# W1's splits wait for batch 5, and the planned order of the work is drawn up anew

## The chip, the core and the metric

The kernel runs on one core of one Trainium2 chip. The metric is the device time of one execution in microseconds (us), as the median of three runs. The core's engines are PE (TensorE, matrix products), DVE (VectorE), ACT (ScalarE), POOL (GpSimd) and SP (SyncE), which issues the transfers (DMA). Each engine works its own queue in order; they wait for each other through semaphores.

## What is computed

Attention of 8 batches with 8 heads, 512 tokens and 32 states each, in both directions, then two MLPs on the 4608 results of width 512, all in float32:

```python
scores = scale * np.matmul(x, state.transpose(0, 1, 3, 2))
a = np.exp(scores - scores.max(-1, keepdims=True))
a /= a.sum(-1, keepdims=True) + 1e-09
xread = np.matmul(a, state)
...                                       # the same with state and x exchanged: sread
x = concatenate([xread, sread]) as 8 * (512 + 32) tokens of 512
h = x @ w_in                              # first MLP, 512 -> 1024: W1
solu = h * softmax(h)
ln = (solu - mean) / np.sqrt(var + 1e-06) * g_ln
y = ln @ w_out                            # 1024 -> 512: W2
h = y @ moe2_w_in                         # second MLP, 512 -> 2048: W3
g = h * (1.0 / (1.0 + np.exp(-1.702 * h)))
return g @ moe2_w_out                     # 2048 -> 512: W4
```

## The kernel before

The weights come as 64-bit numbers. `to_f32` (line 440) turns a block of 128 x 512 into float32: a load of 512 KB to a raw tile, two passes on ACT, three on DVE (lines 453, 456 and 458) and an integer addition on POOL (line 460). Products of full precision are made from three products of reduced precision. For that `split` (line 463) copies a tile to a high part `hi` (line 472 on ACT or line 474 on DVE) and subtracts it to a low part `lo` (line 467, on POOL or DVE).

Batches 0 to 7 don't apply W1 to their tokens. Per batch, `attention` transposes x and the state, forms the scores, and takes a softmax over the states: subtraction of maxima m1 (line 595), exponential, sums z1, multiplication (line 602), a transposition to aT (line 605), and a split of aT to `ahi`, `alo` (line 609). The state is multiplied by W1 (`state_w1`, line 566 on PE, split to `vhi`, `vlo`, lines 656 and 657), which uses W1 as float32 and not its splits. So the first product of the first MLP (`mlp1`) of a batch is `ahi`, `alo` against `vhi`, `vlo` (lines 431 to 433 on PE). The other softmax, over tokens, begins with lines 575 to 585 and line 620. Line 710 takes the row maximum of h, line 712 the exponential, line 714 the product u, and lines 724 and 725 scale it. The output product with W2 takes `zhi`, `zlo` (`z_T`, lines 766 to 774; `z_turn`, line 755, from batch 3 on).

What comes from the other direction, 256 tokens of state reads, is batch 8. For these alone W1 is split, to eight pairs `hi_w1s`, `lo_w1s`. Meanwhile W3 is prepared for seven products per block in place of eight (`prepare_up`): four conversions, sums of blocks, seven splits, and stores of these to DRAM; from there the second MLP, 400 us and later, loads them.

The order is not that of the code. Each piece of work is a step with an engine or a choice of engines, a cost, and for some a due time (`key`). A planner runs once, on paper: it passes due times back along the dependences, keeps a time for each engine, and picks the next step among those whose inputs and buffers are there, by the earliest start and then by the earliest due time. Constants say how far ahead loads may go (`LOOK`, `LEAD`), how many buffers stay free (`KF`, `KR`, `RK`, `KEEP`), when a second engine is preferred (`MARGIN`, `LOAD`), how long an early step may be passed over (`WAIT`), and the due times of the parts (`W1DUE`, `ATT`, `M1A`, `M2A`, `SLOT` and others). The instructions are then issued to each engine in the order so found. The chip has no part in it, and waits are real semaphore waits.

The splits of W1 have a due time near batch 7, but nothing keeps the planner from taking them when an engine has nothing more urgent by its own reckoning:

```python
W1s[k, f] = split(W1[k, f], f"w1s_{k}_{f}", b * SLOT - 10 + k + KD * f)
```

Float32 tiles of 128 x 512 share 71 buffers, raw tiles of W1 seven, raw tiles of the other weights two.

Of the kernel before, what the change touches and what calls it, by code (L numbers as in the profile page):

```python
# [15 lines left out]
ALU = mybir.AluOpType  # L16
# [6 lines left out]
ZB = 3  # L23
XD = 3
AHEAD = 30.092
KF = 10.181
LOOK = 27.681
KR = 0.745
STEPS = 13.000
LATEV = 99  # L30
HEADS = 1.060
W1S = 20.477
ATT = -0.468
ZL = 7.738
M1B = -7.631
VST = 25.191
RK = 8
LEAD = 62.849
KEEP = 5
PP = 1.33  # L40
FIRST = "dz"

# [42 lines left out]
class Plan:  # L85
# [88 lines left out]
    def plan(self):  # L174
# [19 lines left out]
        while ready:  # L194
# [4 lines left out]
            for s in ready:  # L199
                e0 = s.eng[0][0]  # L200
                if e0 == "pe" and s.key > front + AHEAD:
                    continue
                if e0 == "dma" and s.due > front + (LEAD if s.keep else LOOK):
                    continue
# [5 lines left out]
                for k, n in need.items():  # L210
# [115 lines left out]
            self.late.release()  # L326


WAIT = 43.673
W1DUE = -10.782  # L330
MARGIN = 19.804
M1A = -3.168
M1S = 14.618
M2A = 48.714
M2S = 3.142
A1 = 4.656
DMAQ = 0
STQ = "dma"
WARM = 7
LD = 1.875  # L340
LA = -0.409
LOAD = dict(dve=LD, act=LA)
COLD = 18.042
IDLE = 2.200
XRAW = 1
BUS = 347350.590

BUS0 = 170067.709
BUS0T = 8.428
PAIR = 14.200  # L350
HOLDM = 2.261
HOLDW = 9.169
HOLD = dict(m=HOLDM, w=HOLDW)


@with_exitstack
def attention_solu_gelu(ctx: ExitStack, tc: tile.TileContext, x, state, w1, w2, g_ln, w3, w4, out):
    nc = tc.nc
    B, H, S, D = x.shape
# [8 lines left out]
    KD = DM // P  # L368
# [4 lines left out]
    scale = 1.0 / float(D) ** 0.5  # L373
    NX = B * NS
    PSUM = bass.MemoryType.PSUM
    SLOT = 40.392

    const = ctx.enter_context(tc.tile_pool(name="const", bufs=1))
    slot_p = ctx.enter_context(tc.tile_pool(name="slots", bufs=1))
# [5 lines left out]
    do, tl = pl.do, pl.tile  # L385
# [21 lines left out]
    def POOL(c):  # L407
        return [("pool", c)]
# [28 lines left out]
    TOP = 122879.9921875  # L437
    TINY = 2.0 ** -15

    def to_f32(src, name, due, after=(), keep=0, kind="r"):  # L440

        raw = tl(kind, [P, 512, 2], U32, f"raw_{name}")
        do(ACT(.1) if kind == "d" and DMAQ else DMA(), lambda e: e.dma_start(out=raw().rearrange("p f w -> p (f w)").bitcast(U64), in_=src),
           writes=[raw], key=due - 4, nbytes=P * 4096, after=after)
        w = tl("s", [P, 512], F32, f"w_{name}")

        def u():
            return w().bitcast(U32)  # L450

        do(ACT(.52), lambda e: e.activation(w(), raw()[:, :, 1].bitcast(F32), AF.Abs), [raw], [w], keep=keep)
        do(DVE(.335), lambda e: e.tensor_scalar(w(), w(), TINY, TOP, op0=ALU.max, op1=ALU.min), [w], [w])
        do(ACT(.52), lambda e: e.activation(raw()[:, :, 0], raw().bitcast(U16)[:, :, 1], AF.Copy, scale=2.0 ** -13),
           [raw], [raw])
        do(DVE(.335), lambda e: e.tensor_scalar(u(), u(), 3, 0x3FFFFFF8, op0=ALU.logical_shift_left,
                                                op1=ALU.bitwise_and), [w], [w])
        do(DVE(.6), lambda e: e.scalar_tensor_tensor(out=u(), in0=raw()[:, :, 1], scalar=0xC0000000, in1=u(),  # L458
                                                     op0=ALU.bitwise_and, op1=ALU.bitwise_or), [raw, w], [w])
        do(POOL(1.23), lambda e: e.tensor_tensor(u(), u(), raw()[:, :, 0], op=ALU.add), [w, raw], [w], key=due)  # L460
        return w

# [51 lines left out]
    def attention(b):  # L514
# [734 lines left out]
```

## Time and profile before

| | |
|---|---|
| runs | 1113.74, 1111.53, 1110.18 us |
| median | 1111.53 us |
| profiled execution, its own time | 1111.82 us |
| its span, first to last instruction | 1110.0 us |
| granted clock of TensorE, mean | 0.988 |
| PE busy | 1070.6 us, 96% |
| DVE, ACT, POOL busy | 808.5, 616.2, 248.3 us |

The profiled execution took 1111.82 us, 1.8 more than the span from its first to its last instruction. Busy time is the time in which an engine works on instructions; what is left of a window is idle. A wait is put down to the instruction that released it. A short form such as "x4" says that four like instructions stand one behind the other, with the time from the first's start to the last's end.

### The profile page before, as it was taken

How to read it: one execution, taken by the hardware profiler on the slowest of the kernel's cores; microseconds unless marked ns; L12 is line 12 of the kernel's file. 1: busy time of each engine (PE TensorE's matmuls, PEld its weight loads, DVE VectorE, ACT ScalarE, POOL GpSimd, SP SyncE). 2: the span in 40 equal slices, each digit the busy share in tenths (PEclk: the TensorE clock that was granted, in tenths of full speed). 3: DMA queues.
4: the chain of work that ended last, by engine and by line, in shares of the span. 5: the costliest groups of instructions: out<-in, count | busy, mean ns of one | idle time of the engine just before them, and what ended most of it. 6: DMA issues, size and time to landing. Idle time of an engine off the chain costs nothing.

```text
span 1110.0 us, 22067 instructions
## 1 busy us (share of the span) xinstructions
PE 1070.6 (96%) x8255; PEld 966.4 (87%) x8255; DVE 808.5 (73%) x1374; ACT 616.2 (56%) x1111; POOL 248.3 (22%) x212
## 2 busy tenths in 40 slices
PE   6689999999899999999999999999999999999998
PEld 3357777767577789999999999999999999999998
DVE  5999767898878838548866665435498888778874
ACT  6587555667557547557756665545354444444441
POOL 3977432651836502310101110000000000000000
PEclk8899999999999999999999999999999999999999
DMA  7314352866754479998776657479934344434521
GB/s 231 81 51 100 84 111 70 231 153 156 201 114 108 158 210 361 336 365 305 243 240 235 216 205 250 160 256 392 375 107 152 104 126 146 129 108 152 152 78 58
DMA packets 233084, 202.81 MB, mean 183 GB/s; under 512 B 128784, under 2 KB 174864, under 8 KB 232976
## 3 DMA queue, kind: packets, MB, share of 16 engines
q1 hardware_dynamic: 232880, 201.26, 57.8%
q8 instruction: 65, 1.06, 0.4%
q14 instruction: 43, 0.35, 0.1%
q10 hardware_dynamic: 96, 0.13, 0.1%
HBM read 113.25 MB, written 82.84 MB: 177 GB/s over the span
## 4 chain that ended last, share of the span: by engine, by line
PE 79%; DVE 6%; SPq 4%; POOL 4%; DMA 2%; issue 2%; ACT 2%; POOLq 0%; DVEq 0%; ACTq 0%
PE psum L1039 10%; PE psum L1037 10%; PE psum L950 10%; PE psum L1038 10%; PE psum L951 10%; PE psum L949 10%; PE psum L431 5%; PE psum L433 5%; PE psum L432 5%; DMA raw_w<-in_moe_w_in 2%; POOL lo_w3s L467 2%; SPq L745 1%; PE psum L766 1%; PE psum L566 1%; DVE w_w L458 1%
## 5 line engine op out<-in xcount | busy, mean ns | idle before, releaser
L1037 PE MATMUL psum<-w4r,hi_g 128*128 128x256 f32 x896 | 252.2, 282 | 0.0
L1039 PE MATMUL psum<-w4r,lo_g 128*128 128x256 f32 x896 | 252.1, 281 | 0.0
L1038 PE MATMUL psum<-w4r,hi_g 128*128 128x256 f32 x896 | 251.9, 281 | 0.0
L1037 PEld LDWEIGHTS psum<-w4r,hi_g 128*128 128x128 f32 x896 | 169.3, 189 | 0.0
L1038 PEld LDWEIGHTS psum<-w4r,hi_g 128*128 128x128 f32 x896 | 169.3, 189 | 0.0
L1039 PEld LDWEIGHTS psum<-w4r,lo_g 128*128 128x128 f32 x896 | 169.2, 189 | 0.0
L472 ACT CAST hi_g<-a_g 128x512 fp32r<-128x512 f32 x128 | 77.9, 620 | 108.5 <-DVE a_g L819 54.6
L460 POOL TENSOR_TENSOR w_w<-w_w,raw_w 128x512 uint32<-128x512 uint32 x48 | 68.7, 1436 | 295.0 <-DVE w_w L458 188.2
L431 PE MATMUL psum<-zhi,hi_w 128*128 128x512 f32 (+1 forms) x288 | 115.6, 401 | 1.5 <-DVE u L714 1.5
L961 DVE TENSOR_TENSOR c<-psum,u 128x512 f32<-128x512 f32 x64 | 44.1, 690 | 92.5 <-PE psum L951 57.3
L433 PE MATMUL psum<-zhi,lo_w 128*128 128x512 f32 (+1 forms) x288 | 110.1, 382 | 0.0
L896 DVE TENSOR_TENSOR lo_g<-a_g,hi_g 128x512 fp32r<-128x512 f32 x128 | 86.0, 687 | 16.9 <-PE psum L1039 8.3
L472 ACT CAST hi_g<-gr 128x512 fp32r<-128x512 f32 x104 | 63.0, 619 | 47.4 <-PE psum L1038 21.8
L933 ACT ACTIVATE t<-c 128x512 f32<-128x512 f32 x96 | 60.5, 632 | 46.6 <-DVE c L961 43.0
L896 DVE TENSOR_TENSOR lo_g<-gr,hi_g 128x512 fp32r<-128x512 f32 x104 | 71.0, 687 | 13.9 <-ACT hi_g L472 8.3
L432 PE MATMUL psum<-zlo,hi_w 128*128 128x512 f32 (+1 forms) x208 | 78.2, 376 | 0.0
L431 PEld LDWEIGHTS psum<-zhi,hi_w 128*128 128x128 f32 x288 | 54.5, 189 | 23.3 <-issue 9.2
L433 PEld LDWEIGHTS psum<-zhi,lo_w 128*128 128x128 f32 x288 | 54.4, 189 | 11.2
L950 PE MATMUL psum<-lo_x,w3r_2h 128*128 128x256 f32 x224 | 63.0, 281 | 0.0
L950 PE MATMUL psum<-lo_x,w3r_3h 128*128 128x256 f32 x224 | 63.0, 281 | 0.0
L951 PE MATMUL psum<-hi_x,w3r_3l 128*128 128x256 f32 x224 | 63.0, 281 | 0.0
L951 PE MATMUL psum<-hi_x,w3r_0l 128*128 128x256 f32 x224 | 62.9, 281 | 0.0
(233 smaller groups left out, 3004.4 us busy)
## 6 DMA issues: line engine op xcount, KB each, us to landing
g<-t SPq DMA_DIRECT2D x136, 256.0 KB, 3.7
gr<-g SPq DMA_DIRECT2D x136, 256.0 KB, 3.3
w4r<-w4k SPq DMA_DIRECT2D x56, 256.0 KB, 5.3
raw_w<-in_moe_w_in SPq DMA_DIRECT2D x24, 512.0 KB, 5.7
raw_w<-in_moe_w_out SPq DMA_DIRECT2D x24, 512.0 KB, 4.9
xb<-scr SPq DMA_DIRECT2D x34, 256.0 KB, 5.0
scr<-x SPq DMA_DIRECT2D x16, 512.0 KB, 4.0
out<-oc SPq DMA_DIRECT2D x32, 256.0 KB, 2.7
```

The costliest lines, as they stand in the source:

```text
L431: nc.tensor.matmul(o, lhi, rhi, start=first, stop=False)
L432: nc.tensor.matmul(o, lhi, rlo, start=False, stop=False)
L433: nc.tensor.matmul(o, llo, rhi, start=False, stop=last)
L460: do(POOL(1.23), lambda e: e.tensor_tensor(u(), u(), raw()[:, :, 0], op=ALU.add), [w, raw], [w], key=due)
L472: e.copy(o, i)
L896: do(DVE(.68), lambda e: e.tensor_tensor(flat_(lo), flat_(t), flat_(hi), op=ALU.subtract), [t, hi], [lo], key=due)
L949: nc.tensor.matmul(o, wh()[:, k, cut], hi()[:, k, :], start=first and not mi + k, stop=False, **OPEN)
L950: nc.tensor.matmul(o, wh()[:, k, cut], lo()[:, k, :], start=False, stop=False, **OPEN)
L951: nc.tensor.matmul(o, wl()[:, k, cut], hi()[:, k, :], start=False, stop=bool(mi and k), **OPEN)
L1037: nc.tensor.matmul(o, hi()[:, mi, cut], wt[:, 0], start=first, stop=False, **OPEN)
L1038: nc.tensor.matmul(o, hi()[:, mi, cut], wt[:, 1], start=False, stop=False, **OPEN)
L1039: nc.tensor.matmul(o, lo()[:, mi, cut], wt[:, 0], start=False, stop=2 * j + mi == NM - 1 and u == 1, **OPEN)
```

## The change

Three edits. The function `split` gets a list of steps that its high part must wait for, and W1's splits are given the last product of batch 5's first MLP (`last` holds the last product of each batch, and B is 8). The last addition of `to_f32` can be put on a choice of engines, and both constants that say so name POOL, as before. And 28 of the planner's constants have other values, of which three stand here.

```diff
-LOOK = 27.681
+LOOK = 37.674
-WAIT = 43.673
+WAIT = 31.914
-MARGIN = 19.804
+MARGIN = 14.062
...
+ADD = ("pool",)
+ADD1 = ("pool",)
...
-    def to_f32(src, name, due, after=(), keep=0, kind="r"):
+    def to_f32(src, name, due, after=(), keep=0, kind="r", add=ADD):
...
-        do(POOL(1.23), lambda e: e.tensor_tensor(u(), u(), raw()[:, :, 0], op=ALU.add), [w, raw], [w], key=due)
+        do([(q, dict(pool=1.23, dve=.6)[q]) for q in add], lambda e: e.tensor_tensor(u(), u(), raw()[:, :, 0], op=ALU.add),
+           [w, raw], [w], key=due)
...
-    def split(w, name, due, shape=(512,), pair=None, low=(("pool", 1.23), ("dve", .6))):
+    def split(w, name, due, shape=(512,), pair=None, low=(("pool", 1.23), ("dve", .6)), after=()):
...
-        do([("act", .52), ("dve", .335)], lambda e: copy(e, hi(), w()), [w], [hi])
+        do([("act", .52), ("dve", .335)], lambda e: copy(e, hi(), w()), [w], [hi], after=after)
...
-                    W1s[k, f] = split(W1[k, f], f"w1s_{k}_{f}", b * SLOT - 10 + k + KD * f)
+                    W1s[k, f] = split(W1[k, f], f"w1s_{k}_{f}", b * SLOT - 10 + k + KD * f, after=[last[B - 3]])
```

The changed lines shift the numbers of those behind them by two or three: line 460 of before is line 462, 467 is 470, 595 is 598, 602 is 605, 609 is 612, 724 and 725 are 727 and 728.

Both kernels have 4468 steps, and nearly all keep their engine; it is their order that differs. Three places of POOL's queue show it. The first is the start of batch 0's softmax and the second half of W1 (`w_w1_k_f` is block k of half f; `s1_0_0` is batch 0's softmax, its first half). Before:

```order
L595 TENSOR_TENSOR s1_0_0_375<-s1_0_0_375,m1_0_0_471 128x512
L595 TENSOR_TENSOR s1_0_1_384<-s1_0_1_384,m1_0_1_479 128x512
L467 TENSOR_TENSOR lo_w1s_0_0_512<-w_w1_0_0_339,hi_w1s_0_0_473 128x512
L467 TENSOR_TENSOR lo_w1s_1_0_521<-w_w1_1_0_354,hi_w1s_1_0_486 128x512
L467 TENSOR_TENSOR lo_w1s_2_0_534<-w_w1_2_0_361,hi_w1s_2_0_504 128x512
L467 TENSOR_TENSOR lo_w1s_3_0_553<-w_w1_3_0_386,hi_w1s_3_0_541 128x512
L460 TENSOR_TENSOR w_w1_0_1_414<-w_w1_0_1_414,raw_w1_0_1_312 128x512
L460 TENSOR_TENSOR w_w1_1_1_450<-w_w1_1_1_450,raw_w1_1_1_316 128x512
L460 TENSOR_TENSOR w_w1_2_1_458<-w_w1_2_1_458,raw_w1_2_1_320 128x512
L460 TENSOR_TENSOR w_w1_3_1_508<-w_w1_3_1_508,raw_w1_3_1_372 128x512
L602 TENSOR_TENSOR s1_0_0_375<-s1_0_0_375,z1_0_0_566 128x512
```

The same place after:

```order
L598 TENSOR_TENSOR s1_0_0_383<-s1_0_0_383,m1_0_0_463 128x512
L598 TENSOR_TENSOR s1_0_1_394<-s1_0_1_394,m1_0_1_466 128x512
L462 TENSOR_TENSOR w_w1_0_1_451<-w_w1_0_1_451,raw_w1_0_1_309 128x512
L462 TENSOR_TENSOR w_w1_1_1_454<-w_w1_1_1_454,raw_w1_1_1_311 128x512
L462 TENSOR_TENSOR w_w1_2_1_459<-w_w1_2_1_459,raw_w1_2_1_316 128x512
L462 TENSOR_TENSOR w_w1_3_1_515<-w_w1_3_1_515,raw_w1_3_1_380 128x512
L605 TENSOR_TENSOR s1_0_0_383<-s1_0_0_383,z1_0_0_538 128x512
L605 TENSOR_TENSOR s1_0_1_394<-s1_0_1_394,z1_0_1_543 128x512
L612 TENSOR_TENSOR alo0_0_577<-aT0_0_561,ahi0_0_563 128x512
L612 TENSOR_TENSOR alo0_1_587<-aT0_1_573,ahi0_1_583 128x512
```

The four low parts between the subtractions (line 595, now 598) and the additions of W1's second half are gone, and the low part of batch 0's softmax, `alo0`, stands directly behind the multiplications.

The second is the first block of W3 (`w_w3_0010` is a converted part of it, `u3_2` a row tile of batch 3). Before, the first two additions stand behind batch 4's `alo`:

```order
L609 TENSOR_TENSOR alo4_0_2234<-aT4_0_2216,ahi4_0_2225 128x512
L725 TENSOR_SCALAR u3_2_2043<-u3_2_2043,sml3_2_2033 128x1024
L609 TENSOR_TENSOR alo4_1_2261<-aT4_1_2228,ahi4_1_2237 128x512
L460 TENSOR_TENSOR w_w3_0010_2038<-w_w3_0010_2038,raw_w3_0010_1917 128x512
L460 TENSOR_TENSOR w_w3_0011_2083<-w_w3_0011_2083,raw_w3_0011_1926 128x512
L724 TENSOR_TENSOR sml3_3_2199<-sml3_3_2199,half_p_80 128x1
L725 TENSOR_SCALAR u3_3_2244<-u3_3_2244,sml3_3_2199 128x1024
```

After, they stand among the scalings of batch 2:

```order
L727 TENSOR_TENSOR sml2_2_1606<-sml2_2_1606,half_p_80 128x1
L728 TENSOR_SCALAR u2_2_1632<-u2_2_1632,sml2_2_1606 128x1024
L462 TENSOR_TENSOR w_w3_0010_1703<-w_w3_0010_1703,raw_w3_0010_1695 128x512
L462 TENSOR_TENSOR w_w3_0011_1750<-w_w3_0011_1750,raw_w3_0011_1697 128x512
L470 TENSOR_TENSOR lo_w3s3_00_1818<-w_w3_0011_1750,hi_w3s3_00_1811 128x512
L727 TENSOR_TENSOR sml2_3_1774<-sml2_3_1774,half_p_80 128x1
L728 TENSOR_SCALAR u2_3_1798<-u2_3_1798,sml2_3_1774 128x1024
L462 TENSOR_TENSOR w_w3_0000_1816<-w_w3_0000_1816,raw_w3_0000_1772 128x512
```

The block moved ahead by one to two batches. The third is batch 6's softmax and W3's second block (`lo_w3s0_10` is the low part of the first of its seven sums). Before:

```order
L460 TENSOR_TENSOR w_w3_1001_3058<-w_w3_1001_3058,raw_w3_1001_3015 128x512
L595 TENSOR_TENSOR s1_6_0_3079<-s1_6_0_3079,m1_6_0_3163 128x512
L595 TENSOR_TENSOR s1_6_1_3087<-s1_6_1_3087,m1_6_1_3188 128x512
L467 TENSOR_TENSOR lo_w3s0_10_3212<-w_w3_1000_3050,hi_w3s0_10_3170 128x512
L467 TENSOR_TENSOR lo_w3s1_10_3228<-w_w3_1001_3058,hi_w3s1_10_3186 128x512
L467 TENSOR_TENSOR lo_w3s2_10_3237<-a4_w3_10_3204,hi_w3s2_10_3221 128x512
L467 TENSOR_TENSOR lo_w3s4_10_3252<-a1_w3_10_3181,hi_w3s4_10_3191 128x512
L467 TENSOR_TENSOR lo_w3s5_10_3270<-a2_w3_10_3199,hi_w3s5_10_3206 128x512
L467 TENSOR_TENSOR lo_w3s6_10_3278<-a3_w3_10_3230,hi_w3s6_10_3244 128x512
L602 TENSOR_TENSOR s1_6_0_3079<-s1_6_0_3079,z1_6_0_3242 128x512
L602 TENSOR_TENSOR s1_6_1_3087<-s1_6_1_3087,z1_6_1_3274 128x512
```

After:

```order
L470 TENSOR_TENSOR lo_w3s5_10_3037<-a2_w3_10_2978,hi_w3s5_10_2997 128x512
L470 TENSOR_TENSOR lo_w3s2_10_3051<-a4_w3_10_3012,hi_w3s2_10_3026 128x512
L470 TENSOR_TENSOR lo_w3s6_10_3069<-a3_w3_10_3023,hi_w3s6_10_3043 128x512
L598 TENSOR_TENSOR s1_6_0_3082<-s1_6_0_3082,m1_6_0_3124 128x512
L598 TENSOR_TENSOR s1_6_1_3088<-s1_6_1_3088,m1_6_1_3136 128x512
L605 TENSOR_TENSOR s1_6_0_3082<-s1_6_0_3082,z1_6_0_3164 128x512
L470 TENSOR_TENSOR lo_w1s_0_0_3238<-w_w1_0_0_346,hi_w1s_0_0_3230 128x512
L605 TENSOR_TENSOR s1_6_1_3088<-s1_6_1_3088,z1_6_1_3222 128x512
L727 TENSOR_TENSOR sml5_0_2886<-sml5_0_2886,half_p_80 128x1
L727 TENSOR_TENSOR sml5_1_2989<-sml5_1_2989,half_p_80 128x1
L727 TENSOR_TENSOR sml5_2_3102<-sml5_2_3102,half_p_80 128x1
L612 TENSOR_TENSOR alo6_0_3293<-aT6_0_3248,ahi6_0_3266 128x512
```

All low parts of the block stand ahead of batch 6's subtractions now, and one of W1's (`lo_w1s_0_0`) stands between its two multiplications.

## Rows read from the trace of the kernel before

**Rows 1.** The page's first part: busy time, share of the span, instructions.

```profile
PE 1070.6 (96%) x8255; PEld 966.4 (87%) x8255; DVE 808.5 (73%) x1374; ACT 616.2 (56%) x1111; POOL 248.3 (22%) x212
```

**Rows 2.** Windows: start:end, length; busy PE, PEld, DVE, ACT, POOL; PEclk, DMA, GB/s.

```profile
0.00:25.00 25.00, 15.13 (x131) 8.60 (x133) 13.25 (x34) 16.16 (x32) 5.64 (x10) 0.80 0.81 242
25.00:50.00 25.00, 15.22 (x61) 5.40 (x58) 24.42 (x36) 13.29 (x27) 23.53 (x18) 0.87 0.41 103
50.00:100.00 50.00, 44.69 (x305) 32.51 (x304) 45.76 (x86) 41.66 (x83) 35.21 (x30) 0.96 0.20 65
100.00:199.00 99.00, 98.08 (x706) 74.06 (x704) 73.79 (x151) 57.36 (x108) 42.43 (x43) 1.00 0.40 89
199.00:231.00 32.00, 28.97 (x168) 20.91 (x168) 28.65 (x47) 22.18 (x42) 16.80 (x15) 1.00 0.81 219
231.00:274.00 43.00, 41.25 (x278) 30.12 (x277) 38.47 (x71) 28.85 (x56) 16.73 (x16) 1.00 0.74 168
274.00:303.00 29.00, 24.38 (x173) 15.68 (x173) 27.34 (x50) 16.97 (x33) 25.82 (x21) 0.94 0.65 187
303.00:400.00 97.00, 96.62 (x537) 75.68 (x536) 71.75 (x122) 60.09 (x108) 42.65 (x37) 1.00 0.49 123
400.00:500.00 100.00, 100.00 (x792) 97.31 (x791) 53.87 (x82) 58.07 (x103) 19.89 (x13) 1.00 1.01 345
500.00:1100.00 600.00, 600.00 (x5068) 600.00 (x5067) 430.07 (x698) 301.56 (x526) 19.57 (x14) 1.00 0.57 193
1100.00:1110.00 10.00, 6.31 (x54) 6.10 (x52) 1.18 (x3) 0.00 (x0) 0.00 (x0) 0.91 0.22 54
```

**Rows 3.** PE's waits, 0 to 100 us: total us, times, longest.

```profile
PE psum L620 <- ACT e2t L582: 7.2, 1, 7.2
PE psum L566 <- POOL w_w L460: 5.2, 4, 4.5
PE psum L431 <- DVE u L714: 3.2, 3, 2.2
```

**Rows 4.** POOL's timeline: start, us, instruction, count, idle before.

```profile
28.59 5.69 POOL L467 TENSOR_TENSOR lo_w1s<-w_w,hi_w1s 128x512 fp32r<-128x512 f32 x4
35.24 6.28 POOL L460 TENSOR_TENSOR w_w<-w_w,raw_w 128x512 uint32<-128x512 uint32 x4 [0.96 <-DMA st<-in_state]
```

**Rows 5.** DVE's timeline in the same stretch.

```profile
23.89 5.02 DVE L453 TENSOR_SCALAR w_w<-w_w 128x512 f32<-128x512 f32 x4
28.83 5.73 DVE L456 TENSOR_SCALAR w_w<-w_w 128x512 uint32<-128x512 uint32 x4
34.48 4.65 DVE L458 SCALAR_TENSOR_TENSOR w_w<-raw_w,w_w 128x512 uint32<-128x512 uint32 x4
```

**Rows 6.** Instructions on W1's low parts: least, median, most ns, first and last.

```profile
L432 PE MATMUL psum<-lo_w1s,hi_xs x16: 388/394/404, 371.7 to 390.1; 128*128 128x512 f32 x16
L467 POOL TENSOR_TENSOR lo_w1s<-w_w,hi_w1s x8: 1270/1448/1472, 28.6 to 54.2; 128x512 fp32r<-128x512 f32 x8
```

**Rows 7.** Line 456, the second pass of a conversion, same columns.

```profile
L456 DVE TENSOR_SCALAR w_w<-w_w x48: 378/427/1499, 11.1 to 671.1; 128x512 uint32<-128x512 uint32 x48
```

**Rows 8.** DVE's groups, 75 to 105 us: busy, mean ns, idle before.

```profile
L710 DVE TENSOR_REDUCE sml<-psum 128x1 f32<-128x1024 f32 x3 | 3.7, 1217 | 0.3 <-PE psum L433 0.3
...
L575 DVE STREAM_TRANSPOSE s<-psum 128x512 f32<-128x512 f32 x2 | 1.4, 716 | 0.3 <-ACT e2t L582 0.3
```

**Rows 9.** Window 199 to 231 us, instructions on tiles w_w alone.

```profile
199.00:231.00 32.00, 1.95 (x32) 0.60 (x32) 8.95 (x11) 3.21 (x5) 9.08 (x7) 1.00 0.81 219
```

**Rows 10.** POOL's timeline in batch 6's softmax.

```profile
280.60 2.98 POOL L595 TENSOR_TENSOR s<-s,m 128x512 f32<-128x512 f32 x2
283.53 3.44 POOL L467 TENSOR_TENSOR lo_w3s<-w_w,hi_w3s 128x512 fp32r<-128x512 f32 x2
286.94 4.98 POOL L467 TENSOR_TENSOR lo_w3s<-a_w,hi_w3s 128x512 fp32r<-128x512 f32 x4
...
298.90 2.39 POOL L725 TENSOR_SCALAR u<-u,sml 128x1024 f32<-128x1024 f32 x2
```

More of the change, by code (lines that the diff above doesn't have):

```diff
@@ L25 @@
 AHEAD = 30.092
-KF = 10.181
-LOOK = 27.681
-KR = 0.745
-STEPS = 13.000
+KF = 7.648
+LOOK = 37.674
+KR = 1.064
+STEPS = 14.103
 LATEV = 99
 HEADS = 1.060
[L32 to L35, printed above, removed]
+W1S = 26.323
+ATT = 1.067
+ZL = 7.757
+M1B = -7.403
 VST = 25.191
-RK = 8
-LEAD = 62.849
-KEEP = 5
+RK = 3
+LEAD = 23.973
+KEEP = 6
+ADD = ("pool",)
+ADD1 = ("pool",)
 PP = 1.33
@@ L326, in emit @@
             self.late.release()
-WAIT = 43.673
-W1DUE = -10.782
-MARGIN = 19.804
[L332 to L336, printed above, removed]
+WAIT = 31.914
+W1DUE = -6.816
+MARGIN = 14.062
+M1A = -4.431
+M1S = 20.090
+M2A = 55.785
+M2S = 4.848
+A1 = 6.428
 DMAQ = 0
@@ L339 @@
 WARM = 7
-LD = 1.875
-LA = -0.409
+LD = 2.914
+LA = -0.539
 LOAD = dict(dve=LD, act=LA)
-COLD = 18.042
-IDLE = 2.200
+COLD = 13.349
+IDLE = 1.393
 XRAW = 1
 BUS = 347350.590
[L348 to L351, printed above, removed]
+BUS0 = 120538.582
+BUS0T = 9.714
+PAIR = 14.310
+HOLDM = 1.514
 HOLDW = 9.169
@@ L375, in attention_solu_gelu @@
     PSUM = bass.MemoryType.PSUM
-    SLOT = 40.392
+    SLOT = 43.045
     const = ctx.enter_context(tc.tile_pool(name="const", bufs=1))
@@ L1135, in get1 @@
     def get1(k, f):
-        W1[k, f] = to_f32(rows(w1, k, f), f"w1_{k}_{f}", W1DUE + 2 * (k + KD * f), kind="d")
+        W1[k, f] = to_f32(rows(w1, k, f), f"w1_{k}_{f}", W1DUE + 2 * (k + KD * f), kind="d", add=ADD1)
     get1(0, 0)
```

## The prediction

> **What bounds the kernel now.** I began with the busy times [rows 1]: PE (TensorE) works 1070.6 of 1110.0 us, so at most 39.4 us can be won unless TensorE is given less work or a better clock, and the change alters no matmul. Where those 39.4 us lie is seen in a table of windows [rows 2]; length less PE's busy time is what PE stood idle. From 400 to 1100 us it is nothing: 100.00 of 100 and 600.00 of 600. The last ten hold 3.7 (6.31 busy). The other 35.7 fall into three places: 9.9 + 9.8 + 5.3 = 25.0 in the first 100 us, 3.0 + 1.75 from 199 to 274, and 4.6 from 274 to 303. In each of these DVE (VectorE) or POOL (GpSimd) is nearly full: DVE 24.42 of 25 and POOL 23.53 of 25 from 25 to 50, DVE 28.65 of 32 from 199 to 231, DVE 27.34 and POOL 25.82 of 29 from 274 to 303. From 100 to 199 DVE works 73.79 of 99 and POOL 42.43, and PE stands only 0.9. So this is a kernel in which PE is late only where the two elementwise engines are crowded, and the change can act there alone, by changing what stands in their queues and when.
>
> What PE waits for in the first 100 us [rows 3]: 7.2 us, once, for the first exponential (start-up, behind the first loads; nothing of the change stands ahead of it), 5.2 in four waits for the additions that end W1's conversions, 4.5 of them in one, and 3.2 for mlp1 products that wait for the softmax product u.
>
> The 4.5 us wait is explained by POOL's queue [rows 4]: between batch 0's two subtractions (ahead of 28.59) and the four additions of W1's second half (35.24 to 41.52) stand four low parts lo_w1s, 28.59 to 34.28, 5.69 us, which nothing needs before 371.7 us, when their first product runs [rows 6]. DVE's queue [rows 5] shows the other half: in the same stretch the passes of those conversions take 5.02, 5.73 and 4.65 us for four each, 1.26, 1.43 and 1.16 apiece. The same second pass takes 0.427 us at the median of its 48 and 1.499 at the most [rows 7]: beside a POOL instruction on full tiles DVE is about three times slower, and the longest are as long as one lo_w1s (1.448, rows 6).
>
> **The change part by part.** Three things move; no step is added or dropped (4468 before and after), and the changed additions still run on POOL.
>
> A, the first 100 us. All eight splits of W1 leave: eight low parts by 1.448 = 11.6 us by the median, on POOL [rows 6]. As the first order fence shows, four additions now follow batch 0's subtractions at once. The additions could start when POOL is through with the subtractions, 28.6, but each needs the third pass on DVE, whose last ended at 39.13 (34.48 + 4.65, rows 5). Without lo_w1s beside them the second passes fall from 5.73 towards 4 x 0.427 = 1.7, unless the additions themselves now obstruct the third passes; I reckon the last third pass 1.6 to 3.7 us earlier and take 2.6. Behind it hang sums, aT, ahi and the first mlp1 product. DVE's queue is also reordered: up to batch 1's last value low part it holds 84 instructions in place of 96: at the mean of 25 to 50 us, 24.42 over 36 or 0.68, twelve are 8; seven that leave are small, so 6.5 less. But up to the first z low part of mlp1's output it holds 122 in place of 112: batch 2's softmax start (two transposes by 0.716, two reductions alike), a row maximum by 1.217 and a product u by about as much [rows 8], and two smaller ones, some 7.4 us more, while PE, by the same order, has less to do ahead of batch 2's first product, since output products of batch 0 now stand behind it. So what is won near 37 us is partly lost between 50 and 100, where PE stood 5.3. Best: the four waits of 5.2 go whole, -5. Worst: 7.4 more DVE less the 2.6 and less 2.2 of the wait for u that goes, +3 (rounded up). I take -1.5, the nearer to the 4.5 us row less its return.
>
> B, 199 to 231 us. W3's first prepared block (conversions, sums and seven splits) stands on POOL after batch 4's alo's now and after batch 2's scaling in the changed order (second order fence), that is one and a half batches earlier, between 100 and 199 us. There PE has 0.9 idle in 99 us and DVE a quarter free [rows 2], which hides it. In 199 to 231 the steps on w_w alone are 8.95 us of DVE and 9.08 of POOL [rows 9]. With them gone DVE has 19.7 in 32. PE's 3.0 us then go to about 0.3, the rate of 100 to 199: -2.7; bounds 0 (W1's splits or other steps fill the place) and -4.8 (with the 1.75 up to 274). I take -2.5. If that cover were gone, 8.95 us of DVE in the way would cost what they cost now, about 3. SP's loads of that block come earlier too, where the DMA share is 0.40 instead of 0.81.
>
> C, 274 to 303 us. W3's second block moves ahead of batch 6's subtractions on POOL (third order fence). Now it stands between them and the sums: two low parts, 3.44, and four, 4.98 [rows 10]. PE's 4.6 us are waits for that batch's softmax and the clock falls to 0.94 [rows 2]. Some of W1's splits come into this stretch in exchange: one (1.45) stands between the two sums, and four scalings of batch 5 between alo6_0 and alo6_1, where two (2.39, rows 10) stood. Between -4.6 (all idle goes) and +9.9 (the low parts are late and delay batch 6's first alo by 3.44 + 4.98 + 1.45); nearest to the row of PE's idle, halved for what comes in, -2.
>
> D, 303 to 400 us. W1's splits come here: eight low parts and eight high parts, 11.6 us on POOL in a stretch where POOL has 42.65 of 97 and DVE 71.75, PE waits 0.4 [rows 2]. Between 0 and +3 (PE waits for two low parts of 1.45); taken as +0.5, near the 0.4 of the row.
>
> E, 400 us on. The next MLP's loads keep the DMA queues full (share 1.01, 345 GB/s) and yet PE has no gap in 400 to 500 [rows 2]. SP issues the first inputs of that MLP ahead of 16 small transfers of batch 7 in the new order, not behind them. 0, at worst +3.
>
> Sum: -1.5 - 2.5 - 2 + 0.5 + 0 = -5.5 against the profiled execution's own 1111.82 (span 1110.0 and 1.8 around it) gives 1106.3. That execution lies 0.3 above the median 1111.53, so 1106.0.
>
> The Trainium skill ("SBUF — State Buffer", section "SBUF: two separate sides") has a rule against such a change: the port that DVE and GpSimd share is an exclusive lock, and whoever comes second is blocked for the whole instruction. Rows 7 agree in size: 1.499 is near one 1.448 POOL instruction. By that rule the change only carries the blocking to another stretch, which is rival 3.
>
> **The rivals.**
> 1. DVE takes POOL's place in the first 100 us (A at +3, the rest as forecast): for it, DVE works 24.42 of 25 and 45.76 of 50 there [rows 2] and has 7.4 us more ahead of the first output product; against it, the additions come earlier. 1106.0 + 4.5 = 1110.5.
> 2. The gains are whole: A -5, B -2.7, C -4.6 and D 0: -12.3; and if PE no longer pauses from 25 to 50 us, its granted clock of 0.87 there rises too, 13% of 15.22 busy, -2.0. 1111.8 - 14.3 - 0.3 = 1097. For it, all three idle places have their cause named; against it, each has other work behind it.
> 3. The obstruction moves with the splits: eight POOL instructions block fast DVE ones by 1.499 - 0.427 = 1.07 each in batch 6's and 7's stretch, 8.6 us on a DVE that has 27.34 of 29. With the loss not hidden, 1106.0 + 8.6 = 1114. For it, rows 7; against it, POOL's obstruction costs PE only where DVE is full, and after 303 it has a quarter free.
> 4. Slower: POOL around batch 6. If W3's second block isn't done when batch 6's maxima are there, seven low parts stand ahead of its subtractions instead of behind, and a lo_w1s between its sums. Price 3.44 + 4.98 + 1.45 = 9.87 on batch 6's first alo, and C's -2 is lost: 1106.0 + 2 + 9.9 = 1117.9. It decides if the block's last addition starts later than about 268 us: behind that start stand its own 1.6 (6.28 over 4, rows 4) and seven low parts of 1.45, and the subtractions came at 280.6 [rows 10]. For it, the low parts stand in line on one queue; against it, its loads are put earlier on SP.
>
> **How the numbers follow.** Forecast .42, its own range 1102 to 1109; rival 1 .20, rival 2 .15, rival 3 .08, rival 4 .15. What can be told from no change is 0.3%, 3.3 us: faster is under 1108.2, slower over 1114.9. Faster: .38 of the forecast, .15 of rival 2, .05 of rivals 1 and 3, .58. Slower: .12 of rival 4, .04 of rivals 1 and 3, .16. The same: .26. The range 1098 to 1115 leaves out half of rival 2 and most of rival 4, .19.
>
> **What would show it.** A: no lo_w1s in POOL's first 100 us, W1's second-half additions ending at 37.4 to 39.9 in place of 41.5, PE's wait for them below 3, DVE's second passes nearer 0.43; PE idle in the first 100 us 23.5 in place of 25. B: PE idle below 1 from 199 to 231. C: PE idle about 2.6 in batch 6's stretch; a wait of 5 or more for batch 6's alo means rival 4. D: PE idle below 1 in 303 to 400 and no wait for lo_w1s. E: PE 100% from 400. Wrong it would be if the first 100 us hold more than 28 us of idle, or a new idle stretch opens after 303.

## The result and the profile after

The changed kernel takes 1098.9 us (median of 4, 1098.69 to 1099.08) against 1111.6 of before: ratio 0.9883, 95% interval 0.9868 to 0.9899. Forecast were 1106.0, so the direction was right and the gain, 12.7 us, more than twice the 5.5 of the sum. Timed once more, on another chip for the last experiment, it took 1101.4 beside 1110.8 of before (ratio 0.9913, 0.9897 to 0.9928). So the gain is 9 to 13 us.

The page's first part and the windows of the changed kernel answer to [rows 1, 2]; columns are the same, and the last two windows end with the shorter span.

```profile
PE 1066.1 (97%) x8255; PEld 964.8 (88%) x8255; DVE 803.5 (73%) x1364; ACT 620.2 (57%) x1125; POOL 243.3 (22%) x208
```

```profile
0.00:25.00 25.00, 15.42 (x129) 7.57 (x129) 13.82 (x35) 15.12 (x30) 6.21 (x10) 0.80 0.76 226
25.00:50.00 25.00, 19.86 (x107) 9.23 (x103) 24.01 (x39) 14.57 (x30) 15.70 (x13) 0.93 0.48 120
50.00:100.00 50.00, 43.26 (x357) 32.55 (x351) 48.56 (x99) 40.31 (x83) 35.83 (x33) 0.93 0.44 105
100.00:199.00 99.00, 97.53 (x659) 73.08 (x658) 82.59 (x154) 64.66 (x123) 49.25 (x45) 1.00 0.48 126
199.00:231.00 32.00, 32.00 (x222) 25.03 (x221) 25.17 (x50) 20.61 (x38) 5.36 (x6) 1.00 0.68 145
231.00:274.00 43.00, 41.65 (x281) 30.16 (x281) 39.52 (x72) 29.92 (x57) 26.01 (x20) 1.00 0.69 186
274.00:303.00 29.00, 29.00 (x156) 21.64 (x155) 21.79 (x41) 21.19 (x41) 22.02 (x22) 1.00 0.69 140
303.00:400.00 97.00, 95.23 (x530) 74.26 (x529) 74.50 (x126) 60.28 (x110) 43.61 (x35) 1.00 0.55 154
400.00:500.00 100.00, 98.59 (x827) 97.92 (x826) 55.92 (x82) 61.24 (x108) 19.50 (x13) 1.00 0.96 329
500.00:1087.30 587.30, 587.30 (x4961) 587.30 (x4960) 416.43 (x672) 292.27 (x512) 19.85 (x14) 1.00 0.57 190
1087.30:1097.30 10.00, 6.28 (x54) 6.08 (x52) 1.18 (x3) 0.00 (x0) 0.00 (x0) 0.98 0.22 54
```

In the page, PE's busy time falls from 1070.6 to 1066.1 with the same 8255 instructions, and what is left of the span from 39.4 to 31.2. So of the 12.7 us 8.2 are idle time that is gone and 4.5 are busy time. Of the two only the first repeats: the profile that was taken when the changed kernel was timed once more has a span of 1099.6, of which 31.1 are idle, and PE busy 2.1 less than before.

```profile
PE 1068.5 (97%) x8255; PEld 965.9 (88%) x8255; DVE 803.3 (73%) x1364; ACT 620.7 (56%) x1125; POOL 243.6 (22%) x208
```

Window by window the idle time went: 0 to 100 us 25.0 to 21.5, 100 to 199 0.9 to 1.5, 199 to 231 3.0 to nothing, 231 to 274 1.75 to 1.35, 274 to 303 4.6 to nothing, 303 to 400 0.4 to 1.8, 400 to 500 none to 1.4. The stretch 199 to 303, which was 9.4 us idle, holds 1.35. (The changed kernel is 4 to 14 us ahead there, so a window holds somewhat later work.) From 274 to 303 the granted clock rises from 0.94 to 1.00, which for 24.38 us of work is an estimated 1.5 us; but from 50 to 100 it falls from 0.96 to 0.93. With busy time times the missing share of the clock summed over all windows, the clock takes 8.8 us before and 7.6 after, so it accounts for about 1.2 of the 4.5. Where the rest comes from is not shown.

PE's waits in the first 100 us, answering to [rows 3]: the start costs 5.3 in two waits, for the first transposed x and the exponential, where it was 7.2 in one, but a new wait of 1.9 for sr follows, and the first 25 us are idle for 9.6 as against 9.9; and the additions, 5.2 before, still cost 3.5, in four waits of at most 1.6.

```profile
PE psum L569 <- ACT xT L475: 3.5, 1, 3.5
PE psum L569 <- POOL w_w L462: 3.5, 4, 1.6
...
PE psum L623 <- ACT e2t L585: 1.8, 1, 1.8
```

POOL's timeline there, against [rows 4]: the subtractions are followed by the additions; the second pair of them waits for DVE's third passes (line 460), and they end at 36.76, 4.8 us earlier than before.

```profile
25.75 2.42 POOL L598 TENSOR_TENSOR s<-s,m 128x512 f32<-128x512 f32 x2
29.86 3.04 POOL L462 TENSOR_TENSOR w_w<-w_w,raw_w 128x512 uint32<-128x512 uint32 x2 [1.69 <-DMA xn<-in_x]
33.91 2.85 POOL L462 TENSOR_TENSOR w_w<-w_w,raw_w 128x512 uint32<-128x512 uint32 x2 [1.02 <-DVE w_w L460]
```

The W1 low parts are at 275.7 to 301.7 us now, against [rows 6], and the steps on w_w that filled 199 to 231 ([rows 9]: DVE 8.95, POOL 9.08) are gone from there.

```profile
L470 POOL TENSOR_TENSOR lo_w1s<-w_w,hi_w1s x8: 1285/1320/1340, 275.7 to 301.7; 128x512 fp32r<-128x512 f32 x8
```

```profile
199.00:231.00 32.00, 0.00 (x0) 0.00 (x0) 1.61 (x2) 1.38 (x2) 0.00 (x0) 1.00 0.68 145
```

POOL in batch 6's softmax, against [rows 10]: W3's second block ends its additions at 256.3 and its low parts at 263.5, then POOL is idle for 5.3 us, and the subtractions come at 268.81, where they came at 280.60. They take 2.06 in place of 2.98.

```profile
254.98 1.35 POOL L462 TENSOR_TENSOR w_w<-w_w,raw_w 128x512 uint32<-128x512 uint32 x1 [1.90 <-ACT hi_w3s L475]
256.28 3.00 POOL L470 TENSOR_TENSOR lo_w3s<-w_w,hi_w3s 128x512 fp32r<-128x512 f32 x2
259.24 4.29 POOL L470 TENSOR_TENSOR lo_w3s<-a_w,hi_w3s 128x512 fp32r<-128x512 f32 x3
268.81 2.06 POOL L598 TENSOR_TENSOR s<-s,m 128x512 f32<-128x512 f32 x2 [5.29 <-DVE r L587]
...
287.73 7.60 POOL L470 TENSOR_TENSOR lo_w1s<-w_w,hi_w1s 128x512 fp32r<-128x512 f32 x6
```

What the leads come to is seen from the start of each batch's first mlp1 product in the traces (us, before; then less before):

| start of | before | changed | dep_alone | move_w1 | dep_w3_early | w3_early | dep_w3_early_hold16 | dep_w3ab_early |
|---|---|---|---|---|---|---|---|---|
| batch 0 | 44.9 | -5.3 | -5.8 | -5.8 | -5.0 | -1.2 | -4.9 | -5.9 |
| batch 4 | 203.8 | -3.8 | -6.2 | -6.6 | -3.5 | +4.1 | +0.3 | -6.1 |
| batch 6 | 297.6 | -13.6 | -5.9 | -3.3 | -12.9 | -0.3 | -0.6 | -15.5 |
| batch 7 | 343.0 | -15.3 | -7.0 | -2.1 | -15.1 | -3.8 | -2.2 | -17.4 |
| second MLP | 426.8 | -15.0 | -4.5 | -1.8 | -10.3 | +4.3 | +1.4 | -16.7 |

The changed kernel wins 5 us in batch 0, keeps 4, and makes ten more between batch 4 and batch 6. The other columns are the experiments that follow.

### The profile page after: what moved, and what is told of

The parts are those of the page before. It is cut to its first block, busy times and chain, and to the rows that moved or that the text cites. A ratio compares the mean times of both kernels' runs of the same rounds, so it can differ in the third digit from the quotient of the medians.

```text
span 1097.3 us, 21991 instructions
## 1 busy us (share of the span) xinstructions
PE 1066.1 (97%) x8255; PEld 964.8 (88%) x8255; DVE 803.5 (73%) x1364; ACT 620.2 (57%) x1125; POOL 243.3 (22%) x208
## 4 chain that ended last, share of the span: by engine, by line
PE 77%; DVE 10%; SPq 4%; DMA 3%; ACT 2%; issue 2%; POOL 1%; DVEq 0%; ACTq 0%; POOLq 0%
PE psum L1040 10%; PE psum L1042 10%; PE psum L1041 10%; PE psum L952 10%; PE psum L953 10%; PE psum L954 10%; PE psum L433 5%; PE psum L434 4%; PE psum L435 4%; SPq L748 2%; DVE sml L713 1%; DMA raw_w<-in_moe_w_in 1%; DVE u L717 1%; DVE w_w L455 1%; PE psum L769 1%
## 5 line engine op out<-in xcount | busy, mean ns | idle before, releaser
L952 PE MATMUL psum<-hi_x,w3r_0h 128*128 128x256 f32 x224 | 63.3, 283 | 1.4 <-ACT u L959 1.2
L954 PE MATMUL psum<-hi_x,w3r_2l 128*128 128x256 f32 x224 | 63.1, 282 | 0.0
```

The source lines that it names most:

```text
L952: nc.tensor.matmul(o, wh()[:, k, cut], hi()[:, k, :], start=first and not mi + k, stop=False, **OPEN)
L954: nc.tensor.matmul(o, wl()[:, k, cut], hi()[:, k, :], start=False, stop=bool(mi and k), **OPEN)
```

## The experiments

After the result two things had to be told apart. The change moves 11.6 us of POOL work (theory 2); and it frees buffers (theory 1), which the prediction had not thought of: W1's split tiles are 16 of the 71 float32 buffers, held from 28 to 390 us in before. The rival is that the constants do it, by other orders (theory 3).

**The parts alone.** dep_alone is the kernel before with the wait and none of the constants; const_alone is the changed kernel without the wait:

```diff
-                    W1s[k, f] = split(W1[k, f], f"w1s_{k}_{f}", b * SLOT - 10 + k + KD * f, after=[last[B - 3]])
+                    W1s[k, f] = split(W1[k, f], f"w1s_{k}_{f}", b * SLOT - 10 + k + KD * f)
```

> The constants of before; only W1's splits wait for batch 5's last product, and the planner draws its order anew. Theory 1 (buffers: the 16 tiles that W1's splits hold from about 30 to 390 us keep W3's blocks back, and the wait frees them): in the new order W3's first block moves 20 to 30 PE steps ahead, its second block hardly, so about half of what was won, 1104 to 1107. Theory 2 (POOL: only the 11.6 us of low parts in the first 55 us count): the idle of the first 100 us falls from 25 to about 20, the rest as before, 1106. Theory 3 (the 28 constants bring it): 1110 to 1112.

> The changed constants; W1's splits wait for nothing and stand at 28 to 52 us in the planned order again, and W3's blocks come later than in the changed kernel. Theory 1 (buffers) and theory 2 (POOL): most of the gain is gone, 1107 to 1112. Theory 3 (constants): 1099 to 1102.

The kernel before took 1110.4 to 1111.3 beside all these runs. dep_alone: 1106.9, ratio 0.9951 (0.9928 to 0.9973), within what theories 1 and 2 gave. const_alone: 1120.4, 1.0074 (1.0054 to 1.0095), slower than before and than any theory had it. So the constants without the wait lose 9 us, the wait alone wins 4, and both together win 12.7. Theory 3 falls: the constants don't bring the gain by themselves.

**Buffers or work.** hold16 leaves W1's splits late, as in the changed kernel, but the planner may not use 16 buffers until batch 5's last product:

```diff
+        held = [self.kinds["s"]["free"].pop() for _ in range(HELD)]
...
             order.append(s)
+            if s is self.give:
+                self.kinds["s"]["free"] += [(s.end, j) for _, j in held]
...
+    pl.give = last[B - 3]
     pl.plan()
```

> The changed kernel, but the planner keeps 16 of the 71 float32 buffers back until batch 5's last product, as if W1's splits lay in them; the work of the splits stays late. Theory 1 (buffers): W3's blocks come as late as with the constants alone, 1104 to 1108, idle of 2 us or more from 199 to 303. Theory 2 (POOL's early work): as fast as the changed kernel, 1098 to 1100.

hold16: 1120.9, 1.0076 (1.0049 to 1.0104): as slow as const_alone, where the splits' work is early too, and slower than theory 1 had it. With these constants the buffers carry the whole 20 us or so between const_alone and the changed kernel, and the early work on POOL none that can be measured.

move_w1 does the reverse: the order of before, in which only the 16 steps of the splits are put elsewhere (a table, wrapped here, of steps and the steps ahead of which they go; nothing is planned anew):

```diff
+MOVED = {1660: [1253], 1661: [1255, 1254], 1076: [1257, 1259], 1669: [1261, 1263], 1670: [1265], 1703: [1267],
+         1710: [1256], 1717: [1258], 1220: [1260], 1709: [1262], 1724: [1264, 1266], 1728: [1268]}
...
+            self.order += [self.steps[i] for i in MOVED.get(s.idx, ())]
+            if s.idx not in moved:
+                self.order.append(s)
```

> The order of before word for word, except that the 16 steps of W1's splits are taken out and put where the changed kernel has them; nothing else is planned anew, and all buffers stay as they were. Theory 1 (buffers): little, W3's blocks stay where they were; the first 100 us give 1 to 3 us and batch 6's stretch gets what is put there, 1108 to 1112. Theory 2 (POOL's early work): 1104 to 1107.

move_w1: 1108.3, 0.9970 (0.9953 to 0.9988), within theory 1 and slower than theory 2 had it. This is term A by itself, 3 us. (Its profiled execution, 1111.06, is one of the slower of its ten.) In the table it leads by 6.6 us up to batch 4 and then loses it: its windows show that 199 to 231 is idle for 3.9 (before 3.0) and 274 to 303 for 5.9 (before 4.6). W1's eight high parts, on ACT from 278.7 to 296.3, and five low parts stand there now beside W3's second block; that they cost the difference isn't shown.

```profile
199.00:231.00 32.00, 28.06 (x133) 20.70 (x132) 26.57 (x43) 20.62 (x40) 14.06 (x12) 0.95 0.78 211
274.00:303.00 29.00, 23.06 (x120) 15.01 (x109) 24.17 (x45) 19.74 (x38) 28.90 (x25) 0.88 0.71 200
```

**W3's blocks put forward by hand.** move_w1_w3a and move_w1_w3ab take the first, and the first and second, of W3's blocks to their places in the changed kernel, by the same kind of table with 60 steps each; a second table puts the blocks' tiles into buffers that W1's splits leave free.

> The order of before word for word, except that W1's splits (as in move_w1) and the 60 steps of W3's first block are taken out and put where the changed kernel has them, in buffers that W1's splits left free. Buffers theory: 199 to 231 us, where move_w1 still has 3.9 us of PE idle, falls below 1.5 and the lead over before, which move_w1 holds at 6.6 us up to batch 4 and loses behind it, is kept up to batch 5's end: 1104 to 1106.5. Rival (the constants' other reorderings made the gain): as move_w1, 1107.5 to 1109.

> As the one before, with the 60 steps of W3's second block moved too. Buffers theory: the 5.9 us of idle that move_w1 has from 274 to 303 fall below 3, 1098.5 to 1103, most of the change's gain by three moves in the old order. Rival (the constants' other reorderings): 1105 to 1109.

Both came out slower than the theory and its rival had it: 1111.8 (1.0019, 1.0003 to 1.0036) and 1113.6 (1.0028, 1.0013 to 1.0042). The windows of move_w1_w3a show why:

```profile
100.00:199.00 99.00, 92.41 (x626) 68.14 (x632) 74.22 (x142) 58.55 (x111) 47.95 (x45) 0.98 0.49 128
199.00:231.00 32.00, 30.39 (x178) 22.45 (x163) 22.98 (x39) 19.79 (x37) 4.56 (x5) 1.00 0.50 104
```

199 to 231 gets better, 3.9 idle to 1.6, but 100 to 199, which the prediction took for free, has 6.6 idle, and move_w1 1.1 there. Steps put into a finished order stand ahead of others that PE waits for. The longest wait there, 4.0 us for a product u at 174.77, ends such a chain: a low part of W3 on POOL stands ahead of the scale `sml`, the scaling on DVE waits 2.42 for that, and the product comes behind it.

```profile
170.01 1.27 POOL L476 TENSOR_TENSOR lo_w3s<-a_w,hi_w3s 128x512 fp32r<-128x512 f32 x1 [2.70 <-ACT hi_w3s L481]
171.24 0.55 POOL L733 TENSOR_TENSOR sml<-sml,half_p 128x1 f32<-128x1 f32 x1
...
171.83 1.75 DVE L734 TENSOR_SCALAR u<-u,sml 128x1024 f32<-128x1024 f32 x1 [2.42 <-POOL sml L733]
```

Whether the place of W3's blocks matters could so neither be shown nor refuted; it needed a planner that lays the rest around them.

**W3's blocks put forward by due times.** The blocks' due times are fixed numbers, in a line that the change does not touch. One of the constants, SLOT, the planned length of a batch, shifts the batches' due times behind them. So the same can be done with one line, and the planner orders the rest:

```diff
-            prepare_up(k, q, (160, 230, 310)[n])
+            prepare_up(k, q, (150, 216, 291)[n])
```

dep_w3_early is dep_alone with this line, w3_early the kernel before with it, dep_w3_early_hold16 is dep_w3_early with 16 buffers held as above, and dep_hold16 is dep_alone with them held. In the expectations from here on theory 1 is that the place of W3's blocks brings the gain, theory 2 that the constants' other reorderings do.

> The old constants and the dependence, with W3's blocks due at 150, 216 and 291. In the planned order both blocks stand near their places in the changed kernel, low parts at PE steps 158 to 187 and 266 to 282. Theory 1: 1098 to 1103, most of the gain with none of the 28 constants. Theory 2: no better than the dependence alone, 1105 to 1109.

> The kernel before with W3's blocks due at 150, 216 and 291 and W1's splits early, without the dependence: 16 buffers are taken from 50 us on. The planned order brings the blocks forward, by less (low parts at 177 to 198 and 272 to 289). Buffers theory: the earlier blocks now crowd out other tiles, 1108 to 1120, slower than dep_w3_early by 8 or more. If buffers don't matter: 3 to 6 slower than dep_w3_early, the price of W1's early splits alone.

> The dependence alone with the old constants, but 16 float32 buffers kept back until batch 5's last product. Its planned order has W3's two blocks at the very PE steps of before, with W1's splits late. Buffers theory: the time of move_w1, 1107 to 1110, against 1106.9 of the dependence alone. Rival (early POOL work): 1106 to 1107, no slower than the dependence alone.

> dep_w3_early with 16 float32 buffers kept back until batch 5's last product; the splits' work stays late. If the buffers are what W1's early splits cost: as slow as w3_early, 1114 to 1119, with the first 55 us as quick as in dep_w3_early. If POOL's early work is: 1099 to 1103.

| time (ratio, interval) | W3 due 160, 230, 310 | W3 due 150, 216, 291 |
|---|---|---|
| W1's splits early | before, 1 | w3_early 1118.3 (1.0059, 1.0039 to 1.0079) |
| splits wait, 16 buffers held | dep_hold16 1109.1 (0.9978, 0.9961 to 0.9995) | dep_w3_early_hold16 1114.1 (1.0026, 1.0015 to 1.0037) |
| splits wait | dep_alone 1106.9 (0.9951, 0.9928 to 0.9973) | dep_w3_early 1099.2 (0.9884, 0.9863 to 0.9905) |

With none of the 28 constants the wait and W3's earlier due times together give the changed kernel's whole gain; alone, the wait gives 4 us and the due times lose 7. Of the 19 us between w3_early and dep_w3_early, 15 go with the buffers and 4 with the splits' early work. Each of these kernels is planned anew and differs in many places, and no number of buffers other than 16 was held back; so the 15 us are the price of the order that the planner finds without the 16, not of one block by itself. At W3's old due times the buffers are worth little (1109.1 against 1106.9, intervals overlapping).

How missing buffers cost time is seen at batch 6. Windows 274 to 303 and 303 to 400 of dep_w3_early, then of dep_w3_early_hold16:

```profile
274.00:303.00 29.00, 27.71 (x202) 21.05 (x201) 24.47 (x49) 20.14 (x39) 19.90 (x18) 1.00 0.67 133
303.00:400.00 97.00, 93.29 (x511) 72.38 (x511) 67.81 (x116) 56.43 (x104) 43.49 (x37) 0.98 0.46 129
```

```profile
274.00:303.00 29.00, 23.61 (x178) 16.41 (x179) 25.99 (x49) 20.20 (x41) 23.38 (x20) 0.88 0.65 166
303.00:400.00 97.00, 94.34 (x515) 71.70 (x514) 71.45 (x121) 58.56 (x107) 45.84 (x40) 1.00 0.43 112
```

From 274 to 303 that is 1.3 us idle at full clock against 5.4 at 0.88. In the latter PE's timeline (start, us, instruction, idle before) has one wait of 7.53 us for z (the second of batch 4's four), and DVE's timeline shows what stands ahead of that z:

```profile
279.38 0.80 PE L436 MATMUL psum<-z,hi_w 128*128 128x512 f32 x1 [7.53 <-DVE z L759]
```

```profile
267.57 0.43 DVE L460 TENSOR_SCALAR w_w<-w_w 128x512 uint32<-128x512 uint32 x1
...
269.31 1.68 DVE L462 SCALAR_TENSOR_TENSOR w_w<-raw_w,w_w 128x512 uint32<-128x512 uint32 x1
270.92 0.68 DVE L823 TENSOR_TENSOR a_w<-a_w,w_w 128x512 f32<-128x512 f32 x1
271.52 1.78 DVE L823 TENSOR_TENSOR a_w<-w_w,w_w 128x512 f32<-128x512 f32 x1
273.22 1.75 DVE L823 TENSOR_TENSOR a_w<-w_w,a_w 128x512 f32<-128x512 f32 x1
...
277.59 1.73 DVE L759 SCALAR_TENSOR_TENSOR z<-z,g_sb,zhi 128x512 fp32r<-128x512 f32 x1
```

Conversion passes and sums of W3's second block (lines here are four behind those of before) hold DVE from 267.57 to 274.97; then come batch 6's maxima, and the z that PE needs begins at 277.59. In dep_w3_early DVE has no step of W3 at this point, and the same four z's are done by 269.33:

```profile
262.29 2.46 DVE L755 SCALAR_TENSOR_TENSOR z<-z,g_sb,zhi 128x512 fp32r<-128x512 f32 x2
...
268.13 1.20 DVE L755 SCALAR_TENSOR_TENSOR z<-z,g_sb,zhi 128x512 fp32r<-128x512 f32 x1
```

With 16 buffers fewer W3's block, some 22 tiles, begins later in the planned order, and falls into batch 6's softmax and the z's beside it, which need DVE too. In that order the second block's low parts stand at PE steps 266 to 282 in dep_w3_early, 272 to 288 with the buffers held. In the traces all seven of them run between 231 and 274 us in dep_w3_early, but only three begin there with the buffers held (windows on the tiles lo_w3s alone; busy POOL):

```profile
231.00:274.00 43.00, 10.53 (x7) 1.00 0.72 193
```

```profile
231.00:274.00 43.00, 3.87 (x3) 1.00 0.65 155
```

**Undone in the changed kernel.** after_w3_late only puts the due times back in proportion to SLOT:

```diff
-            prepare_up(k, q, (160, 230, 310)[n])
+            prepare_up(k, q, (171, 245, 330)[n])
```

> The changed kernel, with one edit: W3's three blocks are due at 171, 245 and 330 in place of 160, 230 and 310. In its planned order the second block's low parts stand at PE steps 270 to 298 again (261 to 281 in the changed kernel, 291 to 299 before), the first block's at 173 to 209 (142 to 165). Theory 1 (the place of W3's blocks between 199 and 303 us is what the surplus comes from): idle and slow clock of that stretch come back, 1104 to 1108. Theory 2 (it comes from the other reorderings that the constants bring, W3 being hidden either way, as move_w1_w3ab hints): 1098 to 1101.

1113.8, 1.0018 (1.0004 to 1.0033): the whole gain is gone, more than theory 1 had. From 274 to 303:

```profile
274.00:303.00 29.00, 22.80 (x170) 16.30 (x170) 26.80 (x46) 19.11 (x36) 27.38 (x23) 0.82 0.59 167
```

6.2 us idle, at a clock of 0.82, where the changed kernel has none at 1.00.

**Other sizes.** dep_slot_look has dep_alone's code with SLOT and LOOK of the changed kernel; after_b6 is the changed kernel with `last[B - 2]` in place of `last[B - 3]`.

> The old constants and the dependence, and two of the 28 constants: SLOT, the planned length of a batch, 43.045, and LOOK, how far ahead loads are planned, 37.674. These two bring W3's blocks to low parts at 142 to 171 and 262 to 282, as in the changed kernel. Theory 1: 1098 to 1103. Theory 2: 1105 or more.

> The changed kernel with W1's splits behind batch 6's last product and not batch 5's; W3's blocks keep their places. Buffers theory: batch 6's stretch and before stay as fast (idle 0 from 274 to 303), the splits now crowd the stretch before 371 us where batch 8 needs them: 1098 to 1103. If the splits in batch 6's stretch were what costs, 1097 to 1098.

dep_slot_look: 1106.3, 0.9944 (0.9922 to 0.9965), as theory 2 had it, though W3's blocks are in place. Its idle time from 199 to 303 is 2.7, but the early batches come later too: from 50 to 100 it has 9.5 idle (before 5.3), and batch 4 starts 2.2 us later than in before, where dep_alone leads by 6.2. So W3's place isn't enough by itself.

```profile
50.00:100.00 50.00, 40.46 (x275) 29.41 (x274) 45.77 (x79) 39.99 (x81) 35.34 (x31) 0.90 0.30 79
```

after_b6: 1109.5, 0.9986 (0.9969 to 1.0003), 8 to 11 slower than the changed kernel and outside both forecasts. It is as fast up to batch 7; from 303 to 400 it has 6.5 us idle and DVE 80.33 of 97 busy. The later the splits, the more they stand beside batch 7's work.

**A faster version.** dep_w3_early loses 5 of its 15.1 us of lead after batch 7 begins. dep_w3ab_early leaves W3's third block at 310, (150, 216, 310); after_w3c_late puts the third block of the changed kernel to 325.

> dep_w3_early with W3's third block due at 310 again (150, 216, 310), since dep_w3_early leads before by 15.1 us when batch 7 begins and by 10 when the second MLP does, with 3.7 us of idle from 303 to 400. If the third block crowds batch 7's stretch: 1094 to 1098, faster than the changed kernel. If it is hidden there: 1098 to 1100.

> The changed kernel with W3's third block due at 325 in place of 310, which moves its low parts from PE steps 365 to 384 to 368 to 396; all before stays. If the third block crowds batch 7's stretch: 1095 to 1098. If not: 1098 to 1101.

dep_w3ab_early: 1095.9, 0.9862 (0.9847 to 0.9877). It keeps its lead, 16.7 us when the second MLP begins, and idles 2.0 us from 303 to 400 in place of 3.7:

```profile
303.00:400.00 97.00, 95.00 (x524) 75.29 (x524) 66.39 (x114) 56.55 (x103) 40.88 (x36) 1.00 0.51 142
```

after_w3c_late: 1101.0, 0.9906 (0.9889 to 0.9922), no faster than the changed kernel: what that loses behind 303 us isn't won back by moving the third block alone. Side by side:

> The changed kernel beside dep_w3ab_early on the same chip: 1097 to 1100.

> dep_w3ab_early beside the changed kernel on the same chip: if the constants carry something of their own beyond W3's place, no faster than the changed kernel; if they don't, 1094 to 1097, some 3 us faster.

1101.4 (0.9913, 0.9897 to 0.9928), slower than the 1097 to 1100 expected, and 1095.3 (0.9858, 0.9839 to 0.9876), as expected: the version with the wait, two due times and none of the constants beats the changed kernel by some 6 us, and the intervals don't touch.

## Why the prediction was wrong

The reading of the profile held: PE was late in three places, DVE and POOL were full there, and the idle time that went came from these, with nothing from 500 us on. What failed are sizes, those of A and C and that of PE's busy time, which the sum left as it was; and behind them the cause of W3's earlier place was missed.

- A, forecast -1.5: the idle time of the first 100 us fell by 3.5. The last third pass ends at 34.38 in place of 39.13, 4.8 us earlier where 2.6 was taken, and the additions at 36.76, earlier than the 37.4 to 39.9 expected; yet PE's wait for them is 3.5, not below 3. DVE's second passes take 3.3 us for four (1.94 for three and 1.39), less than 5.73 and more than the 1.7 hoped for. By itself (move_w1) the term is worth 3 us. That some is given back between 50 and 100 was right (1.4 us more idle there); move_w1 gives back more, between batch 4 and batch 7, for a cause that isn't shown.
- B, -2.5: -3.0 in 199 to 231 and -0.4 to 274, right in size. Its cover was not: moved by hand, the block costs 5.5 us of idle from 100 to 199 (move_w1_w3a against move_w1); planned anew, as in the changed kernel and dep_w3_early, it costs 0.6 to 0.9 there.
- C, -2, is the step that failed first: "nearest to the row of PE's idle, halved for what comes in". The whole 4.6 went, and the clock of this stretch came back. What comes in is hidden: six low parts stand behind the last alo (287.73, 7.60), where DVE has 21.79 of 29 and PE no wait. The halving rested on no row. Nor are the 4.6 us "waits for that batch's softmax": of PE's waits from 274 to 303 in before, the two longest are for stT and z, and the one for alo is 0.6.

```profile
PE psum L566 <- ACT stT L472: 1.4, 1, 1.4
PE psum L432 <- DVE z L755: 1.2, 1, 1.2
PE psum L431 <- DVE vlo L657: 0.9, 1, 0.9
...
PE psum L433 <- POOL alo L609: 0.6, 1, 0.6
```

- PE's busy time was a term at nothing, "the change alters no matmul". It fell by 4.5, and by 2.1 in the second profile of the changed kernel. Some 1.2 of the 4.5 are the clock, which [rows 2] show at 0.94 in C's stretch and which the sum left out; the rest stays open.
- D and E, +0.5 and 0: the idle from 303 to 500 rose by 2.8, to two waits of 1.6 and 1.2 and a small one; these losses were forecast too small, and the signs that the prediction gave for them (idle below 1 to 400, none behind) did not come.

```profile
PE psum L623 <- DVE s L578: 1.6, 1, 1.6
PE psum L952 <- ACT u L959: 1.2, 1, 1.2
PE psum L952 <- DVE c L964: 0.2, 1, 0.2
```

With the busy time the terms measure -3.5 + 0.6 - 3.4 - 4.6 + 1.4 + 1.4 - 4.5 = -12.6, which is the span's -12.7 but for rounding. Against the sum, A and C account for 4.6 us of what it lacks, the busy time for 4.5, and D and E for 2.3 the other way.

The cause: the prediction treated the wait as 11.6 us of POOL work that goes elsewhere, and took W3's earlier place as given by the new order, two things to be added. The experiments show that they hang together: a split that is done early holds its two tiles until it is used, and with the 16 buffers held back W3's earlier due times lose the gain (1114.1 against 1099.2). No row shown here names a buffer that is missing; the names and counts in the code do.

The rivals: number 2 (gains whole, 1097) is nearest, 1.9 us off, but in part by luck: C went whole, A gave 3.5 and not 5, D and E lost 2.8 and not nothing, and its clock term of 2.0 in the first 100 us isn't there (the clock takes 6.8 us before and 7.5 after, by the windows). The fall in busy time made up for these. Number 1 did not come out (DVE has 48.56 of 50 from 50 to 100 and PE 1.4 us more idle, but 4.6 less before). Number 3, the port: the eight low parts now run from 275.7 to 301.7 and PE waits for nothing there, and DVE has room, 21.79 of 29; whether they slow it isn't shown, but the price of 8.6 isn't there. Number 4: its decision point was "later than about 268"; the last addition began at 254.98.

The longest second pass before, 1.499 us, is near a low part's 1.448 and so agrees with the Trainium skill's rule of the exclusive port ("SBUF — State Buffer", section "SBUF: two separate sides"), and no run here decides more of it. Hold16 and const_alone, equal in time, say that with these constants the early POOL work was not the price.

## What to carry to other kernels

When a step is moved or made to wait, count what it holds, not only what it does: write down from when to when its tiles take buffers, and who could not start for want of them. Holding those buffers back in the changed kernel is an experiment of five lines that tells the two apart. Where two edits each do little or harm, try them together before judging either: here +7 and -4 made -12.

## What was not expected of the hardware

POOL's instructions too took longer where DVE was fuller: the two subtractions of batch 6 took 2.98 us where DVE works 27.34 of 29 and 2.06 in the changed kernel, a low part of W1 1.448 at the median at 28 to 54 us (DVE 24.42 of 25 from 25 to 50) and 1.320 at 276 to 302 (DVE 21.79 of 29). That the one causes the other isn't shown. And the same 8255 PE instructions kept PE busy for 4.5 us less in one profile of the changed kernel and 2.1 less in another, of which the granted clock explains only a part.
